# Four v loads issued by GpSimd with a cast in the transfer, in a fused linear-attention and snake-MLP kernel

## The chip, the cores and the metric

The kernel runs on one core of one Trainium2 chip. The metric is the time of one execution on the device in microseconds (us); the median of several executions is compared. TensorE is called PE, VectorE DVE, ScalarE ACT, GpSimd POOL and SyncE SP. SP does nothing but issue transfers (DMAs).

## What is computed

There are two parts, one feeding the other. The first is a linear attention with decay over 4 batches, 8 heads, 768 positions and a head size of 64; the second is a feed-forward network with the snake activation on all 3072 tokens.

```python
# attention; lam: one decay per head
for each block of positions:
    intra = ((q @ k.T) * Dmask) @ v            # Dmask[i, j] = lam ** (i - j) for i >= j, else 0
    inter = (q * lam ** (i + 1)) @ kv_state
    out[block] = intra + inter
    kv_state = lam ** block * kv_state + (k * lam ** (block - 1 - j)).T @ v
# feed-forward, x: [3072, 512]
h = x @ w_in                                   # [3072, 2048]
s = sin(alpha * h)
g = h + s * s / (alpha + 1e-9)
y = g @ w_out                                  # [3072, 512], float32
```

All inputs and the output are float32 in DRAM.

## The kernel before, in words

**Attention.** The 768 positions of a batch are cut into 6 blocks of 128 rows, so there are 24 steps `s` (4 batches of 6). A step loads q, k and v as tiles of 128 rows by 8 heads by 64 (`load_one`, L531, one transfer of 256 KB each, all issued by SP at L543, into the float32 rings `q32`, `k32`, `v32` of six buffers each). A row of such a tile is gathered from eight runs of 64 floats (256 B) in DRAM, one for each head. For the first nine steps (`NPQ`) q has its rows in another order, so that its runs are 1 KB long. Then:

- `prep` (L636) multiplies k and q by powers of lam and writes bfloat16 tiles (`k{s}` at L641, `q{s}` at L647 or L650), on DVE or POOL.
- `T{s}` transposes both on PE (L678, L681) into PSUM, and a copy `tc{s}` brings them to `qkT`; later steps transpose by a DMA instead (`DT{s}`).
- `S{s}` multiplies q with k (L699) into `A_ps`, and DVE multiplies by the mask (`mask{s}`, L703).
- `prep_v` (L659) casts v from `v32` into the bfloat16 ring `v2` of five buffers: `v{s}`, through the helper at L619. This runs on the engine that the table `ENG` names: v0 and v2 on DVE, v1 and v3 on ACT, v4 on POOL.
- `O{s}` adds the state's part (L721, from `Zs`) and the part of this block (L725), `x{s}` copies the result to `xT`, `Z{s}` (L745) updates the state with k and v, and `zs{s}` copies it to `Zs`.

**Feed-forward.** Six chunks of four steps (512 tokens) each. `A{c}.{m}` (L770) is one of 16 groups of 128 hidden columns of chunk c: matmuls, then the sine on ACT (L776), a square `sq` (L781 or L782) on POOL, DVE or ACT, and a fused multiply-add on DVE (L785) into `gT`. A group needs the weights of its columns and the `x` of all four steps of its chunk. `B{c}.{s4}.{m4}` (L801) is a quarter of the second product for one step's 128 tokens. The weights come in sixteen blocks of 512 KB, `w0` to `w7` of w_in and `w8` to `w15` of w_out (`w_block`, L621): a load on SP (L631) into a ring `wst` of five float32 buffers, and a cast `wc{j}` at L619 to bfloat16 on POOL, DVE or ACT.

**Order.** Three things set it. `LOADS` is the order in which SP issues the loads; it begins

```python
    "k0 q0 v0 k1 q1 k2 q2 k3 q3 v1 v2 q4 v3 w0 k4 w1 q5 w2 w3 w4 w5 k5 w6 w7 w8 w9 v4 w10 w11 k6 q6 q7 w12 "
```

`SCRIPT` is the order of PE's work: the attention of steps 0 to 3 with a few idle matmuls (`w1`, `warm`, L842) between them, then the first chunk `A0.0`, `A0.1`, with T4 and S4 among them, and so on. For DVE, ACT and POOL the program makes its own plan: each operation is recorded with what it reads and writes and with an expected duration, and `schedule` (L216) goes through them in expected time. For each engine it takes the operation that can begin first, among those of equal time the one of higher priority, and then the one that PE needs soonest:

```python
                    k = (t, o.prio, o.need, o.idx)
                    if c is None or k < c[0]:
                        c = (k, o, dur)
```

An operation that may run on several engines goes where it is expected to end first, unless `ENG` names an engine for its tag. Transfers are planned by a model of three queues (`Transfers`, L116) that share the DMA engines when more than one of them is busy. `emit` (L355) then writes each engine's instructions in the planned order, with semaphore waits where an operation depends on another. The instructions of an engine run in that order.

POOL starts with the constants (`consts`, L546): one small transfer of lam (`lam_sb`, L565), then five selects that make the identity and mask tiles (`ident`, `identP`, `identf`, `maskP`, `mask`) and three iotas. `mask` is read from step 9 on only; the first nine steps use `maskP`.

Of the kernel before, what the change touches and what calls it, by code (L numbers as in the profile page):

```python
# [38 lines left out]
)  # L39
BIAS_DVE, BIAS_ACT, BIAS_W = (0.3, 0.3, 0.3)  # L40
NPQ, NW, FETCH = 9, 5, 1.2
ENG = {
    "k0": "DVE",
    "k1": "DVE",
# [122 lines left out]
class Program:  # L167
# [10 lines left out]
    def add(self, engs, fn, dur=0.0, reads=(), writes=(), slot=None, work=0.0, after=(), prio=0, tag="",  # L178
            insts=0):
        if isinstance(engs, str):  # L180
            engs = ((engs, dur),)
        elif tag in ENG:
            engs = tuple(x for x in engs if x[0] == ENG[tag])
            call = fn
            fn = lambda e: call(e, ENG[tag])
        op = Op(engs, fn, len(self.ops))
# [236 lines left out]
def bass_lightning_attn__then__act_snake_kernel(  # L423
# [25 lines left out]
    RC = 5  # L449
# [6 lines left out]
    with es:  # L456
# [3 lines left out]
        def ring(name, n, shape, dt):  # L460
            return [sb(f"{name}_{i}", shape, dt) for i in range(n)]
# [10 lines left out]
        v2 = ring("v2", RC, [128, H, D], BF16)  # L472
# [45 lines left out]
        rec = P.add  # L518
# [10 lines left out]
        loads = {}  # L529

        def load_one(nme, s):  # L531
            src, dst = {"k": (k, k32), "q": (q, q32), "v": (v, v32)}[nme]
            b, n, r = s // NB, s % NB, s % RL
            work = 1.19
            d = dst[r][:, :, :]
            if nme == "q" and s < NPQ:
                a = bass.AP(q.tensor, b * H * S * D + n * BL * D,
                            [[4 * D, 32], [2 * S * D, 4], [S * D, 2], [1, 4 * D]])
                d = bass.AP(dst[r], 0, [[H * D, 128], [4 * D, 2], [1, 4 * D]])
                work = 0.74  # L540
            else:
                a = src[b, :, n * BL:(n + 1) * BL, :].rearrange("h p d -> p h d")
            loads[nme, s] = rec("SP", lambda e: e.dma_start(d, a), 0, writes=[f"{nme}32.{r}"],  # L543
                                slot=f"{nme}{r}", work=work, tag=f"L{nme}{s}")

# [72 lines left out]
        def copy_of(e, name, out_ap, in_ap):  # L618
            return e.copy(out_ap, in_ap) if name == "ACT" else e.tensor_copy(out_ap, in_ap)  # L619
# [37 lines left out]
                    tag=f"DT{s}")  # L657

        def prep_v(s):  # L659
            r, c = s % RL, s % RC  # L660
            rec((("ACT", 0.61), ("POOL", 0.74, 0.2), ("DVE", 0.52, 0.3)),
                lambda e, name: copy_of(e, name, v2[c][:, :, :], v32[r][:, :, :]),
                reads=[f"v32.{r}"], writes=[f"v2.{c}"], tag=f"v{s}")
# [41 lines left out]

        def att_O(s, own):
            prep_v(s)
            n, c, j, jq = s % NB, s % RC, s % 2, s % NQ
            if not own:
# [141 lines left out]
        def more_loads():  # L851
            while queue and (queue[0][0] == "w" or queue[0][1] < RL or (queue[0][0], queue[0][1] - RL) in used):
                if queue[0][0] == "w":
                    w_block(queue.pop(0)[1])
                else:
                    load_one(*queue.pop(0))
# [4 lines left out]
        for what in SCRIPT.split():  # L861
            a = what[0]
# [56 lines left out]
```

## Time and profile before

| | |
|---|---|
| median of 8 runs | 220.18 us (219.75 to 220.71) |
| profiled execution | 220.69 us |
| its span, first to last instruction | 218.9 us |
| PE busy | 205.0 us (94%) |
| DVE busy | 148.4 us (68%) |
| ACT busy | 136.5 us (62%) |
| POOL busy | 62.4 us (29%) |
| moved by DMA | 37.76 MB, mean 173 GB/s |
| SP's queue (q1), share of the 16 engines | 67.0% |
| GpSimd's queue (q0), share of the 16 engines | 0.2%, 32 packets |

A busy share is an average over stages that have different limits; what a change in one stage is worth is read from that stage. A transfer's row on SP, ACT or POOL is its issue alone; the data land later. In the profile's tables "releaser" or "<-" names what an engine waited for. The stretches below are given in us from the start of the span.

### The profile page before, as it was taken

How to read it: one execution, taken by the hardware profiler on the slowest of the kernel's cores; microseconds unless marked ns; L12 is line 12 of the kernel's file. 1: busy time of each engine (PE TensorE's matmuls, PEld its weight loads, DVE VectorE, ACT ScalarE, POOL GpSimd, SP SyncE). 2: the span in 40 equal slices, each digit the busy share in tenths (PEclk: the TensorE clock that was granted, in tenths of full speed). 3: DMA queues.
4: the chain of work that ended last, by engine and by line, in shares of the span. 5: the costliest groups of instructions: out<-in, count | busy, mean ns of one | idle time of the engine just before them, and what ended most of it. 6: DMA issues, size and time to landing. Idle time of an engine off the chain costs nothing.

```text
span 218.9 us, 3772 instructions
## 1 busy us (share of the span) xinstructions
PE 205.0 (94%) x1483; PEld 101.5 (46%) x1510; DVE 148.4 (68%) x227; ACT 136.5 (62%) x232; POOL 62.4 (29%) x73
## 2 busy tenths in 40 slices
PE   5885897999999999999999999999999999999995
PEld 1353443445544545445454544455444444444453
DVE  3588596956797875689898867887473778536002
ACT  2665699723689855788868855876734777524020
POOL 4262657450437821238254214010000000000000
PEclk9999999999999999999999999999999999999999
DMA  4999999999999999998999999331101110012023
GB/s 85 259 266 290 337 327 348 336 262 275 253 292 210 232 207 202 259 252 156 238 193 222 224 167 252 73 92 9 48 3 48 48 48 3 0 48 96 0 99 144
DMA packets 94034, 37.76 MB, mean 173 GB/s; under 512 B 82352, under 2 KB 89024, under 8 KB 94016
## 3 DMA queue, kind: packets, MB, share of 16 engines
q1 hardware_dynamic: 90352, 31.33, 67.0%
q10 hardware_dynamic: 3632, 6.17, 8.1%
q8 instruction: 12, 0.20, 0.4%
q0 software_dynamic: 32, 0.00, 0.2%
q14 instruction: 6, 0.05, 0.1%
HBM read 27.28 MB, written 6.29 MB: 153 GB/s over the span
## 4 chain that ended last, share of the span: by engine, by line
PE 81%; DMA 7%; SPq 6%; DVE 2%; issue 2%; POOL 1%
PE m_ps L801 37%; PE m_ps L770 33%; DMA wst<-in_moe_w_in_dram 7%; SPq L543 6%; PE A_ps L699 3%; PE A_ps L725 2%; PE m_ps L823 2%; DVE gT L785 2%; PE m_ps L725 1%; POOL w L619 1%; PE A_ps L721 1%; PE Z_ps L745 1%; PE m_ps L721 1%; POOL u L782 0%; PE A_ps L681 0%
## 5 line engine op out<-in xcount | busy, mean ns | idle before, releaser
L770 PE MATMUL m_ps<-xT,w 128*128 128x512 bf16 x369 | 89.9, 379 | 4.4 <-POOL w L619 1.6
L801 PE MATMUL m_ps<-w,gT 128*128 128x512 bf16 x358 | 87.0, 379 | 1.2 <-issue 0.6
L776 ACT ACTIVATE t<-m_ps,alpha_sb 128x512 bf16<-128x512 f32 x96 | 64.8, 685 | 34.4 <-PE m_ps L770 33.7
L785 DVE SCALAR_TENSOR_TENSOR gT<-u,r_sb,m_ps 128x512 bf16<-128x512 bf16 x96 | 69.8, 744 | 9.5 <-ACT u L781 4.5
L770 PEld LDWEIGHTS m_ps<-xT,w 128*128 128x128 bf16 x384 | 35.5, 98 | 44.2 <-POOL w L619 1.8
L801 PEld LDWEIGHTS m_ps<-w,gT 128*128 128x128 bf16 x368 | 34.6, 98 | 41.0 <-DVE gT L785 0.7
L782 DVE TENSOR_TENSOR u<-t 128x512 bf16<-128x512 bf16 x40 | 17.6, 441 | 19.7 <-ACT t L776 19.5
L781 ACT ACTIVATE u<-t 128x512 bf16<-128x512 bf16 x45 | 28.1, 630 | 1.2
L703 DVE TENSOR_TENSOR S_m<-A_ps,mask 128x1024 bf16<-128x1024 f32 x15 | 18.3, 1223 | 6.3 <-PE A_ps L699 6.1
L619 ACT COPY osb<-m_ps 128x512 f32<-128x512 f32 x18 | 10.5, 584 | 14.2 <-PE m_ps L801 14.1
L782 POOL TENSOR_TENSOR u<-t 128x512 bf16<-128x512 bf16 x11 | 11.4, 1039 | 24.5 <-ACT t L776 24.5
L641 POOL TENSOR_TENSOR qk<-k,Lk 128x512 bf16<-128x512 f32 x11 | 11.9, 1083 | 17.4 <-DMA k<-in_k_dram 17.4
L650 POOL TENSOR_TENSOR qk<-q,Lq 128x512 bf16<-128x512 f32 x11 | 13.1, 1198 | 8.8 <-DMA q<-in_q_dram 8.8
L619 DVE COPY osb<-m_ps 128x512 f32<-128x512 f32 x5 | 3.5, 692 | 14.1 <-PE m_ps L801 14.1
L619 ACT CAST Zs<-Z_ps 64x256 bf16<-64x256 f32 x27 | 9.9, 365 | 4.6 <-PE Z_ps L745 3.1
L641 DVE TENSOR_TENSOR qk<-k,Lk 128x512 bf16<-128x512 f32 x13 | 10.1, 776 | 3.5 <-ACT Lk L561 2.6
L842 PE MATMUL m_ps<-zeros,ident 128*128 128x512 bf16 x27 | 9.7, 491 | 2.5 <-POOL ident L583 2.5
L619 POOL CAST w<-wst 128x1024 bf16<-128x1024 f32 x9 | 9.5, 1056 | 7.6 <-DMA wst<-in_moe_w_in_dram 7.6
L703 DVE TENSOR_TENSOR S_m<-A_ps,maskP 128x1024 bf16<-128x1024 f32 x9 | 11.0, 1217 | 0.7 <-PE A_ps L699 0.7
L647 POOL TENSOR_TENSOR qk<-q,L 128x512 bf16<-128x512 f32 x8 | 8.6, 1074 | 9.7 <-DMA q<-in_q_dram 6.3
L699 PE MATMUL A_ps<-qkT 64*128 64x128 bf16 x192 | 9.5, 219 | 1.4 <-DVE S_m L703 1.0
L699 PEld LDWEIGHTS A_ps<-qkT 64*128 64x128 bf16 x192 | 5.4, 94 | 10.0 <-issue 6.7
(73 smaller groups left out, 125.0 us busy)
## 6 DMA issues: line engine op xcount, KB each, us to landing
k<-in_k_dram SPq DMA_DIRECT2D x24, 256.0 KB, 5.0
q<-in_q_dram SPq DMA_DIRECT2D x24, 256.0 KB, 5.3
v<-in_v_dram SPq DMA_DIRECT2D x24, 256.0 KB, 5.1
out_dram<-osb ACTq DMA_DIRECT2D x23, 256.0 KB, 2.8
wst<-in_moe_w_in_dram SPq DMA_DIRECT2D x8, 512.0 KB, 7.6
wst<-in_moe_w_out_dram SPq DMA_DIRECT2D x8, 512.0 KB, 7.6
qkT<-qk SPq DMA_TRANSPOSE x15, 4.0
out_dram<-osb ACTq DMA_DIRECT2D x1, 128.0 KB, 1.8
```

Of the source, the lines that this page charges most:

```text
L543: loads[nme, s] = rec("SP", lambda e: e.dma_start(d, a), 0, writes=[f"{nme}32.{r}"], slot=f"{nme}{r}", work=work, tag=f"L{nme}{s}")
L619: return e.copy(out_ap, in_ap) if name == "ACT" else e.tensor_copy(out_ap, in_ap)
L641: rec(two, lambda e, _: e.tensor_tensor(k2[c], k32[r][:, :, :], Lk_b, ALU.mult), reads=[f"k32.{r}", "Lk"], writes=[f"k2.{c}"], tag=f"k{s}")
L650: rec(two, lambda e, _: e.tensor_tensor(q2[c], q32[r][:, :, :], Lq_b, ALU.mult), reads=[f"q32.{r}", "Lq"], writes=[f"q2.{c}"], tag=f"q{s}")
L699: last = e.matmul(A_ps[:, 4 * h + jp, :], qkT[j][rows, 4 + jp, :], qT(s, rows, jp))
L703: rec("DVE", lambda e: e.tensor_tensor(S_m[j2][:, :, :], A_ps[:, :, :], mask_b, ALU.mult), 1.22, reads=["S0", "S1", "maskP" if s < NPQ els ...
L770: last = e.matmul(m_ps[i][:, 0:n], w1[:, kc, 128 * m:128 * (m + 1)], xT[x][:, kc, 0:n], start=(kc == 0), stop=(kc == NKC - 1))
L776: rec("ACT", lambda e: e.activation(t16[tt][:, 0:n], m_ps[i][:, 0:n], ACTF.Sin, scale=alpha_sb[:, m:m + 1]), 0.27 + 0.41 * f, reads=[f"m.{ ...
L781: return e.activation(u16[tt][:, 0:n], t16[tt][:, 0:n], ACTF.Square)
L782: return e.tensor_tensor(u16[tt][:, 0:n], t16[tt][:, 0:n], t16[tt][:, 0:n], ALU.mult)
L785: rec("DVE", lambda e: e.scalar_tensor_tensor(out=gT[g][:, m, 0:n], in0=u16[tt][:, 0:n], scalar=r_sb[:, m:m + 1], in1=m_ps[i][:, 0:n], op0 ...
L801: last = e.matmul(m_ps[bank][:, :], gT[g][:, m, 128 * s4:128 * (s4 + 1)], w2[:, m, :], start=(m == 0), stop=(m == NM - 1))
```

## The change

For the first four steps (`NSV = 4`) v is no longer loaded as float32 by SP and cast by an engine. Instead POOL issues a transfer that reads the float32 v from DRAM and writes bfloat16 straight into the tile `v2` of that step; the transfer has its own four semaphores (`sv0` to `sv3`). The planner is told 1.4 us of POOL for the issue and the same work on the DMA engines as before. `prep_v` has nothing to do for these steps. SP's list of loads is walked through as before, without v0, v1, v2 and v3. The steps from 4 on are as they were, and `LOADS`, `SCRIPT` and `ENG` are unchanged.

```diff
 NPQ, NW, FETCH = 9, 5, 1.2
+NSV = 4
 ENG = {
...
                 a = src[b, :, n * BL:(n + 1) * BL, :].rearrange("h p d -> p h d")
+            if nme == "v" and s < NSV:
+                loads[nme, s] = rec("POOL", lambda e: e.dma_start(v2[s % RC][:, :, :], a), 1.4, writes=[f"v2.{s % RC}"],
+                                    slot=f"sv{s % RC}", work=1.19, tag=f"L{nme}{s}")
+                return
             loads[nme, s] = rec("SP", lambda e: e.dma_start(d, a), 0, writes=[f"{nme}32.{r}"],
                                 slot=f"{nme}{r}", work=work, tag=f"L{nme}{s}")
...
         def prep_v(s):
+            if s < NSV:
+                return
             r, c = s % RL, s % RC
             rec((("ACT", 0.61), ("POOL", 0.74, 0.2), ("DVE", 0.52, 0.3)),
                 lambda e, name: copy_of(e, name, v2[c][:, :, :], v32[r][:, :, :]),
```

## The prediction

> **What bounds the kernel now.** I read the page's slices first, then the chain of waits, then the busy time by stage, then the rows of the engines that the change touches. The slices show two regimes: TensorE (PE) is at 9 tenths from the eighth slice on, and in the slices before that it is the DMA engines that are full.
>
> ```profile
> PE   5885897999999999999999999999999999999995
> DMA  4999999999999999998999999331101110012023
> GB/s 85 259 266 290 337 327 348 336 262 275 253 292 210 232 207 202 259 252 156 238 193 222 224 167 252 73 92 9 48 3 48 48 48 3 0 48 96 0 99 144
> ```
>
> The chain of waits says which transfers matter. From 14 us to 42 us it is these pieces (start, length, what):
>
> ```profile
> 14.23 7.17 DMA wst<-in_moe_w_in_dram
> 21.40 0.05 issue
> 21.46 1.05 POOL w L619
> ...
> 27.48 7.62 DMA wst<-in_moe_w_in_dram
> 35.09 0.05 issue
> 35.15 1.21 POOL w L619
> 36.36 1.01 POOL u L782
> ```
>
> So the first feed-forward group (A0.0, 22.55) waits for weight block w0, landing at 21.40, and the stall around 37 to 38 us goes back to w7, landing at 35.09. Both transfers were issued over 7 us before they landed: they stand behind everything queued ahead of them. Busy time by stretch (PE, PEld, DVE, ACT, POOL, clock, DMA share, GB/s):
>
> ```profile
> 3.00:5.20 2.20, 2.20 (x7) 0.79 (x6) 0.70 (x3) 0.21 (x1) 0.75 (x4) 1.00 0.77 155
> 5.20:12.00 6.80, 5.77 (x40) 2.44 (x37) 4.22 (x5) 4.05 (x9) 2.11 (x3) 1.00 1.08 259
> 12.00:20.00 8.00, 5.93 (x103) 4.01 (x104) 7.00 (x11) 5.27 (x10) 3.82 (x4) 1.00 1.13 264
> 23.00:28.00 5.00, 4.95 (x36) 2.45 (x36) 3.54 (x6) 4.19 (x7) 2.58 (x3) 1.00 1.03 343
> 54.00:57.00 3.00, 2.84 (x44) 1.86 (x46) 2.56 (x5) 1.32 (x3) 1.66 (x2) 1.00 1.16 224
> ```
>
> Weights run at 343 GB/s (1 KB runs), the q, k and v loads around 55 us at 224 GB/s (all of 256 B runs there), each with the engines full. After 42.2 us PE is busy 171.7 of 176.7 us; what the start wins or loses, the end wins or loses.
>
> **What the Trainium skill says.** "DMA: Bandwidth & Descriptors", section Issuing engines are not separate DMA queues: transfers started by SP, ACT or GpSimd run on the same 16 engines and interleave, so a second issuer saves only issue time. The trace agrees as far as it can: SP needs 0.59 us for the issue of v0, far less than the load's landing time, 5.1 us in the median. The same page, SWDGE vs HWDGE vs iDMA: a cast in the transfer is only possible from GpSimd, where software writes the descriptors. The trace has one such issue, without a cast (lam_sb, 0.77 us). "Perfetto Trace Analysis", DMA Instruction — SWDGE (GPSIMD): the row of such an issue ends when the last descriptor is written, not when data has moved; lam_sb shows it, 0.77 us of row and 4.8 us to landing. "SBUF — State Buffer", section SBUF: two separate sides: a VectorE operation in a two-port mode keeps GpSimd from writing descriptors. No row of before shows this; VectorE's only v cast in the stretch, at 8.52 us, is one that the change removes.
>
> **The change, part by part.** *Removed casts.* v0 and v2 on DVE, v1 and v3 on ACT:
>
> ```profile
> 8.52 0.41 DVE L619 CAST v<-v 128x512 bf16<-128x512 f32 x1
> ...
> 17.40 0.93 DVE L619 CAST v<-v 128x512 bf16<-128x512 f32 x1
> 18.25 1.21 DVE L703 TENSOR_TENSOR S_m<-A_ps,maskP 128x1024 bf16<-128x1024 f32 x1
> ```
>
> ACT's two (0.62 us each) stand in idle stretches. DVE's second one stands ahead of mask3: S3 ended at 17.61, so mask3 could begin about 0.6 us earlier, and with it O3 and x3, which ends at 21.41. But A0.0 begins only after the cast of w0 ends at 22.50: x3 already has 1.1 us of slack. Worth at A0.0: 0.
>
> *Four issues off SP.* They cost SP 0.59, 2.56 for two, and 0.60 us: 3.75 us. w0's issue at 14.23 goes to about 10.5. Its landing isn't set by that but by the engines ahead: 7.17 us lie between the two. Worth by itself: 0. Later SP runs sooner into the ring of five weight buffers (w7 uses the buffer of w2, cast at 26.00 to 27.04); it then waits longer there, with several us of transfers still queued. Cost 0 while that backlog lasts; were it gone, w7 couldn't start before 27.1.
>
> *Four issues on POOL.* POOL is free from 3.74 (end of the mask select) to 7.01 and from 8.05 to 10.56:
>
> ```profile
> 3.46 0.28 POOL L586 TENSOR_SCALAR_AFFINE_SELECT mask<-maskf 128x128 bf16<-128x128 f32 x1
> 7.01 1.04 POOL L647 TENSOR_TENSOR qk<-q,L 128x512 bf16<-128x512 f32 x1 [3.26 <-ACT Lk L561]
> 10.56 1.04 POOL L641 TENSOR_TENSOR qk<-k,Lk 128x512 bf16<-128x512 f32 x1 [2.50 <-DMA k<-in_k_dram]
> ```
>
> The planner takes, of the operations ready at one time, the one that PE needs first; the loads need nothing, so they go behind the maskP select (ends 3.50) and ahead of `mask`, which is used only from step 9 on. Each has 128 x 8 runs, 1,024, against 128 for lam_sb. Price: at least lam_sb's 0.77 us; at most eight times that, 6.2; I take the 1.4 that the diff gives the planner. 3.5 + 4 x 1.4 = 9.1 us, before k2's scaling at 10.56, whose data landed only then. Cost 0; up to 1.75 us each it would be hidden. What stands in the way is q0's scaling at 7.01: the planner, seeing POOL taken, will give it to DVE behind k0. k0 took 1.50 us beside POOL's q0 and k1 alone 0.68, so k0 and q0 in turn on DVE take about 1.4 us where they took 1.5 side by side. T0 (8.71) stays.
>
> *The transfers.* The same 4 x 256 KB are read. A v at 224 GB/s occupies the engines for 262,144 / 224e3 = 1.17 us, four for 4.7 us, all of them before w0 in either kernel. Can a second queue fill gaps? k0 to k4, v0 to v3 at 224 and q0 to q4 (1 KB runs) at 343 GB/s need 9 x 1.17 + 5 x 0.76 = 14.3 us for 3.67 MB: 256 GB/s. The stretches 5.2 to 20 already run at 259 and 264. The gap is before 5.2 us (155 GB/s), and v0 issued at 3.5 comes too late for it: lam_sb landed 4.8 us after its issue. The planner itself assumes that two queues together run 1.09 times as fast; over some 9 us of two queues that would be 0.8 us. A cast's descriptors don't appear in the trace: bounds are 0.8 us gained in all (the planner's factor), and, if each costs twice a plain one because the cast runs in the path, 4.7 us lost. I take 0.
>
> *Order.* POOL's loads take engine turns from k1 to q3. At worst all four v pass ahead of q3, which v1 to v3 followed before: 3 x 1.17 = 3.5 us. q3's scaling goes from 13.90 to about 17.4, T3 from 15.22 to 18.5, and T3 to the end of x3 took 6.2 us with DVE's queue in between, about 4.6 at bare durations (T3 0.60, copy 1.01, S3 0.40, mask3 1.22, O3 0.75, x3 0.59): 23.1, against 22.50 for w0's cast: 0.6 us at worst, and nothing at a fair share, where q3 comes 1 to 2 us later. I take 0. New waits: PE at O0 to O3 waits for the v transfer instead of a cast; behind it stand the next S and T, and DVE's mask after them. O0 (13.84) has several us to spare; O1 to O3 likewise.
>
> *Replanning.* The planner assigns many later operations by its own times, which shift by some tenths; I put that at 0 with 0.4 us either way, half of one scaling or cast (0.7 to 1.0 us on DVE and POOL) coming onto the path or leaving it.
>
> Sum: 0 at the casts, 0 at SP, 0 at POOL, 0 at the engines: the profiled execution of 220.69 us (span 218.9 and 1.8 around it) would come out at 220.7. It lies 0.5 us above the median of the eight runs; against that median the forecast is **220.2 us**.
>
> **The rivals.** *R1, slower: the cast's descriptors are dear on the DMA engines.* Place: the engines before w0 and w7. For: runs of 256 B are already the least efficient kind (224 against 343 GB/s), and the written runs become 128 B. Against: the same number of runs is moved. Price at half as much again: 4 x 0.59 = 2.3 us later at w0 and w7, with nothing between to absorb it (PE idles only 1.7 us from 22.55 to 42.2): 222.5. It decides from 1.28 us a load on (0.44 us in all).
>
> *R2, slower: writing 1,024 descriptors holds POOL.* At 2.5 us each v3's issue ends at 13.5; k2 and q2 come 3 us late, T2 to x3 with them; less 1.1 us of slack and the 0.6 us of the cast gone, A0.0 is 1.3 us late: 221.5. It decides from some 2.3 us each (3.5 + 4 x 2.3 = 12.7, over 10.56 by 1.7 and 0.44). Against: 1.4 is well under that.
>
> *R3, faster: two queues do run better than one.* For: the DMA share goes to 1.13 where packets overlap, so a share of 1 is no ceiling. Against: the even mix rate above. Up to 0.8 us at w0 and w7, and x3 (ahead by 0.6) allows it: 219.4.
>
> *R4: nothing but the replanning*, 219.8 to 220.6; this has the forecast's time and counts with it.
>
> **How the numbers follow.** 0.2% of 220 us, 0.44 us, is about what a measurement of this kernel can tell from no change. Forecast with R4: 0.38, of which 0.28 lie within 0.44 us, 0.04 below and 0.06 above. R1: 0.25. R2: 0.14. R3: 0.23. Faster 0.27, same 0.28, slower 0.45. For 8 in 10: R3's full size and a little replanning give 219.2; R1 at half as much again with 0.3 us of replanning gives 222.8. The forecast's own range is 219.7 to 220.7.
>
> **What would show it.** Right: four POOL issue rows of about 1.4 us from 3.5 to 9.1; q0 on DVE; w0 landing within 0.4 us of 21.40 and w7 of 35.09; x3 ending near 21 and A0.0 near 22.5. R1: the GpSimd queue's share of the engines well over 4 x 1.17 / 219 = 2.1%, w0 and w7 late alike. R2: rows over 2.3 us, k2's scaling late. R3: w0 and w7 both early, and more GB/s from 5 to 20 us. Wrong altogether would be a change that first appears after 45 us.

## The result: slower by 1.1%, and the profile after

| | before | after |
|---|---|---|
| median | 220.04 us (32 runs) | 222.51 us (11 runs, 221.5 to 224.0) |
| ratio | | 1.0108 (95% interval 1.0086 to 1.013) |
| profiled execution | 220.69 us | 221.18 us |
| its span | 218.9 us | 219.3 us |

Each ratio in what follows is to the runs of before made on the same chip beside it. The profiled execution of after is the quickest of its twelve (the median is over the other eleven), so its trace shows where the start changes, not the whole 2.5 us. The slices, in the form in which the prediction shows those of before:

```profile
PE   5666899999999999999999999999999999999994
PEclk9997999999999999999999999999999999999999
DMA  4999999999999999999999999230101110012023
GB/s 89 218 275 329 334 317 337 357 232 246 256 303 204 230 189 188 257 246 198 203 206 199 243 176 223 48 91 11 48 3 48 48 48 3 0 48 96 0 99 143
```

A slice is 5.5 us. The second and third digits of PE were 8 and are now 6: PE does less between 5.5 and 16.4 us; in the fourth slice its clock is down to 7 tenths. The DMA engines are as full as they were, yet GB/s falls in the second slice (259 to 218) and rises in the fourth (290 to 329). The stretches of the start, with the columns of the prediction, say the same: 
```profile
5.20:12.00 6.80, 4.74 (x40) 2.19 (x37) 3.64 (x5) 4.08 (x9) 3.12 (x5) 1.00 1.62 216
12.00:20.00 8.00, 4.58 (x80) 3.30 (x80) 5.32 (x9) 2.34 (x5) 4.59 (x7) 0.94 1.22 300
```

PE was busy for 5.77 and 5.93 us in them and is now for 4.74 and 4.58. The transfers with the cast count in GB/s by what they write, 128 KB, not by the 256 KB they read, so the 216 looks worse than it is. By bytes read (each v counted as 256 KB), before had moved some 4.3 MB by 20 us and after some 4.8 MB. Something arrives earlier, and something later. The chain of waits says which of the two sets the time (start, length, what):

```profile
7.12 8.59 DMA k<-in_k_dram
15.71 0.07 issue
15.78 1.04 POOL qk L646
16.82 1.01 POOL qk L652
17.83 0.04 issue
17.88 0.40 PE m_ps L685 x4
...
18.71 0.22 PE m_ps L728 x4
...
20.54 0.58 PE m_ps L728 x4
...
22.94 0.38 PE m_ps L728 x4
23.32 0.36 PE m_ps L732 x8
23.68 0.02 issue
23.70 0.59 ACT xT L624
24.30 0.14 issue
24.43 1.02 PE m_ps L777 x4
```

Before, the piece that ended last ahead of A0.0 was weight block w0. Now it is k3: landed at 15.7, scaled on POOL (L646), then q3 behind it on the same engine (L652), then T3 (L685) at 17.88. The three rows of L728 are O1, O2 and O3: they stand behind T3 in PE's order, one after another through the state. x3 ends at 24.29, and A0.0 begins at 24.43. POOL's timeline shows the issues and the two scalings (start, length, what, in brackets the idle time before it and what ended it):

```profile
3.48 3.60 POOL L545 DMA_DIRECT2D v<-in_v_dram  x4
...
11.07 1.04 POOL L646 TENSOR_TENSOR qk<-k,Lk 128x512 bf16<-128x512 f32 x1 [3.69 <-DMA k<-in_k_dram]
...
15.78 1.04 POOL L646 TENSOR_TENSOR qk<-k,Lk 128x512 bf16<-128x512 f32 x1 [2.94 <-DMA k<-in_k_dram]
16.78 2.04 POOL L652 TENSOR_TENSOR qk<-q,L 128x512 bf16<-128x512 f32 x2
18.77 1.04 POOL L624 CAST w<-wst 128x1024 bf16<-128x1024 f32 x1
```

The four issues take 0.90 us each and end at 7.08; after the `mask` select POOL idles until k2 lands. The last row is w0's cast: it begins at 18.77, not at 21.46, and A0.0 no longer waits for it. Landings and PE's milestones of the two profiled executions (a landing is the issue plus the time to landing in the DMA view):

| us | before | after | |
|---|---|---|---|
| k2, q2 landed | 10.5, 11.9 | 11.0, 13.4 | +0.5, +1.5 |
| k3, q3 landed | 13.0, 13.8 | 15.7, 16.4 | +2.7, +2.5 |
| T3 begins | 15.22 | 17.88 | +2.7 |
| w0, w7 landed | 21.4, 35.1 | 18.7, 31.9 | -2.7, -3.2 |
| A0.0 begins | 22.55 | 24.43 | +1.9 |
| A0.15 begins | 42.21 | 42.58 | +0.4 |
| A5.15 begins | 199.53 | 199.91 | +0.4 |

So the q and k loads of steps 2 and 3 come later, the weights earlier. A0.0 loses 1.9 us to the first; the second gives 1.5 us back by A0.15, because the wait for w7 is gone. That the median lies 2.5 us over that of before, and this execution only 0.5 us over the profiled one of before, is taken up below.

### The profile page after: what moved, and what is told of

It is laid out like the page before. It is cut to its first block, busy times and chain, and to the rows that moved or that the text cites. A ratio compares the mean times of both kernels' runs of the same rounds, so it can differ in the third digit from the quotient of the medians.

```text
span 219.3 us, 3768 instructions
## 1 busy us (share of the span) xinstructions
PE 204.9 (93%) x1483; PEld 102.1 (47%) x1510; DVE 150.8 (69%) x226; ACT 133.4 (61%) x228; POOL 66.0 (30%) x78
## 4 chain that ended last, share of the span: by engine, by line
PE 84%; DMA 4%; ACT 3%; SPq 3%; DVE 3%; issue 2%; POOL 1%; DVEq 0%
PE m_ps L808 36%; PE m_ps L777 35%; DMA k<-in_k_dram 4%; SPq L548 3%; PE A_ps L706 3%; PE m_ps L732 2%; PE A_ps L732 2%; PE m_ps L830 2%; DVE gT L792 2%; PE m_ps L728 1%; ACT t L783 1%; ACT u L788 1%; PE Z_ps L752 1%; PE A_ps L728 1%; PE m_ps L849 1%
## 5 line engine op out<-in xcount | busy, mean ns | idle before, releaser
L789 DVE TENSOR_TENSOR u<-t 128x512 bf16<-128x512 bf16 x45 | 22.3, 498 | 21.4 <-ACT t L783 21.0
L788 ACT ACTIVATE u<-t 128x512 bf16<-128x512 bf16 x41 | 25.5, 628 | 1.0
L624 ACT COPY osb<-m_ps 128x512 f32<-128x512 f32 x20 | 11.7, 585 | 15.6 <-PE m_ps L808 15.6
L646 POOL TENSOR_TENSOR qk<-k,Lk 128x512 bf16<-128x512 f32 x14 | 14.8, 1065 | 15.9 <-PE Z_ps L752 8.9
L655 POOL TENSOR_TENSOR qk<-q,Lq 128x512 bf16<-128x512 f32 x11 | 12.4, 1131 | 13.2 <-DMA q<-in_q_dram 13.2
L624 DVE COPY osb<-m_ps 128x512 f32<-128x512 f32 x3 | 2.1, 692 | 13.4 <-PE m_ps L808 13.4
L849 PE MATMUL m_ps<-zeros,ident 128*128 128x512 bf16 x27 | 8.9, 454 | 2.5 <-POOL ident L588 2.5
L624 POOL CAST v<-v 128x512 bf16<-128x512 f32 x10 | 6.6, 670 | 15.0 <-DMA v<-in_v_dram 13.7
L624 ACT CAST xT<-m_ps 128x512 bf16<-128x512 f32 x8 | 4.7, 586 | 10.7 <-PE m_ps L732 10.6
```

Of the source, the lines that this page charges most:

```text
L646: rec(two, lambda e, _: e.tensor_tensor(k2[c], k32[r][:, :, :], Lk_b, ALU.mult), reads=[f"k32.{r}", "Lk"], writes=[f"k2.{c}"], tag=f"k{s}")
L655: rec(two, lambda e, _: e.tensor_tensor(q2[c], q32[r][:, :, :], Lq_b, ALU.mult), reads=[f"q32.{r}", "Lq"], writes=[f"q2.{c}"], tag=f"q{s}")
L788: return e.activation(u16[tt][:, 0:n], t16[tt][:, 0:n], ACTF.Square)
L789: return e.tensor_tensor(u16[tt][:, 0:n], t16[tt][:, 0:n], t16[tt][:, 0:n], ALU.mult)
L849: last = e.matmul(m_ps[bank][:, :], ident[:, :], zeros[:, :])
```

## The experiments

TURNS is the theory that follows: the two queues take turns on the DMA engines, the v loads (needed late) pass the k and q loads (needed early), and A0.0 waits for x3. Its rivals are dear casts, the fall of the PE clock (0.94 between 12 and 20 us) and the new plan.

### The same loads without the cast

```diff
-                loads[nme, s] = rec("POOL", lambda e: e.dma_start(v2[s % RC][:, :, :], a), 1.4, writes=[f"v2.{s % RC}"],
+                loads[nme, s] = rec("POOL", lambda e: e.dma_start(d, a), 1.4, writes=[f"v32.{r}"],
...
         def prep_v(s):
-            if s < NSV:
-                return
```

> v0 to v3 are still issued by POOL, but as float32 into v32, and the four casts on DVE and ACT are back. Theory TURNS (the POOL transfers take engine turns from k2, k3 and q3, so T3 comes late): k3's scaling again starts between 14.5 and 16 us, T3 between 17 and 18.5, and the time is 222 to 223.5. Theory DEAR CASTS (the converting descriptors cost the engines more than plain ones): the GpSimd queue's share falls from 3.9% to about 2.2%, k3's scaling starts before 14 us, and the time is 220 to 221.

Measured: 223.54 us, ratio 1.0175 (1.0152 to 1.0199). The casts on DVE and ACT are back here and the plan is another, so the time alone doesn't tell what the cast in the transfer costs. Where the k loads land tells more: DEAR CASTS expected k3's scaling before 14 us, and k3 landed at 17.0. TURNS had the direction, but T3 began at 19.44, later than its 17 to 18.5. POOL's queue in the page of after (packets, MB, share of 16 engines), and the same line of this kernel:

```profile
q0 software_dynamic: 4192, 0.53, 3.9%
```

```profile
q0 software_dynamic: 352, 1.05, 2.3%
```

With the cast each run of 64 numbers is a packet of its own, 128 B written; without it the packets are of some 4 KB. The k2 load on the other queue, issued at 4.2 us in both, landed at 11.0 in after and at 14.8 here, as POOL's scaling of it shows:

```profile
14.90 1.04 POOL L646 TENSOR_TENSOR qk<-k,Lk 128x512 bf16<-128x512 f32 x1 [7.51 <-DMA k<-in_k_dram]
```

The Trainium skill ("DMA: Bandwidth & Descriptors", section Queues, rings and completion order) says that an engine goes round its queues a whole packet at a time. Larger packets on POOL's side would then take more of each round from SP's; the 3.8 us by which k2 came later agree with that, though the transfers alone (below) show far less of it.

### Two loads issued later

```diff
-                                    slot=f"sv{s % RC}", work=1.19, tag=f"L{nme}{s}")
+                                    slot=f"sv{s % RC}", work=1.19, after=[loads["q", 2]] if s > 1 else [], prio=-1 if s > 1 else 0, tag=f"L{nme}{s}")
```

> The change, with v2 and v3 issued by POOL only when q2 has landed. TURNS: with two loads instead of four beside k2 to q3, k3's scaling starts at 13.5 to 14.5 us instead of 15.8, T3 by 16.2, and the time is 219.5 to 221. DEAR CASTS: the same descriptors are spent before w0, the weights land as in the change, and the time is 222 or more. The planner puts k3 on DVE here, which may help T3 by up to 1 us of its own; e4_pins measures that.

Measured: 224.99 us, ratio 1.0245 (1.0223 to 1.0267). The first half of TURNS came true: k3 landed at 13.5 and T3 began at 15.79. The time, for which it had 219.5 to 221 us, did not follow, because v2 and v3 and their consumers came late. In the chain of waits:

```profile
12.67 7.31 DMA v<-in_v_dram
19.98 0.05 issue
20.03 0.40 PE m_ps L728 x4
...
22.18 2.11 issue
24.29 0.59 PE m_ps L728 x4
```

The last two rows are O3: v3, issued at 13.61, landed at 24.2, though the profile doesn't name it as what ended that wait. A0.0 began at 26.18. The two loads took 7.3 and 10.6 us to land, so "later" was too late. The experiment confirms what delays k3 and refutes the cure.

### The PE clock

Eleven more idle matmuls ahead of T2 and T3, in after:

```diff
-    ... S1 t2 w1 o0 S2 t3 w1 o1 ...
+    ... S1 w5 t2 w1 o0 S2 w6 t3 w1 o1 ...
```

> The change, with five and six more idle matmuls (w5, w6) on PE ahead of T2 and T3, where PE stood idle. Theory CLOCK (much of the loss is the half-speed stretch that follows PE's idle gaps at 12.5 to 17.9 us): the granted clock stays at 1.0 until the end, the runs scatter less, and the median comes to 220.5 to 221.5. Theory TURNS ALONE (the late T3 is all of it): the clock may stay up, but the median is 222 to 223.5, the added matmuls (11 at 0.22 us, 2.4 us) filling idle time at best.

Measured: 223.51 us, ratio 1.0171 (1.0149 to 1.0194). The clock was 1.0 in every run, where in after it is 0.983 to 1.0 in the mean of a run. The time did not improve. The plan changed with it, so the trial was repeated with the plan held (below).

### Two scalings put on the engines that had them

k3's scaling back on DVE and q2's on POOL, as before the change:

```diff
 ENG = {
...
+    "k3": "DVE",
+    "q2": "POOL",
```

> The change, with k3 held on DVE and q2 on POOL as in the kernel before. Theory PLAN (the planner's new assignment, k3 and q3 one after the other on POOL, is the main loss): T3 starts 1 us or more earlier than 17.9 and the time is 220 to 221. TURNS: k3 still lands at 15 to 16 us, T3 gains at most the 1 us of q3's waiting behind k3, and the time is 221.5 to 223.

Measured: 221.27 us, ratio 1.0067 (1.0041 to 1.0092). The time lies between the two forecasts. In the profiled execution, the slowest of the six (222.18 us), k3 landed at 15.7 as in after and T3 began at 17.65, only 0.2 us earlier. The two scalings seem to be worth some 0.4%, but not by way of T3.

### The plan of before, kept exactly

Here the planner plans the kernel before. Afterwards the four v loads are put on POOL behind the `maskP` select, their casts are dropped, and the users of a cast wait for the load; every other instruction keeps its engine and its place.

```diff
+    def moved(self, order):
+        by = {o.tag: o for o in order}
+        casts = {by[f"v{s}"]: by[f"Lv{s}"] for s in range(NSV)}
...
+            if o in moved or o in casts:
+                continue
+            out.append(o)
+            if o.tag == "maskP_sel":
+                out += list(casts.values())
...
-        order = self.schedule()
+        order = self.moved(self.schedule())
```

> The four transfers alone: every engine keeps the order and the engine choices that the planner made for the kernel before; only the four loads go to POOL behind the maskP select and the four casts are dropped. TURNS: k3 lands at 15 to 16 us as in the change, T3 starts near 16.8 (k3 on DVE, q3 on POOL), the granted clock halves for 3 to 7 us, and the time is 220.8 to 222. REPLANNING (the new plan is the main loss): the time is at or below the kernel before, 219 to 220.2, since w0 and w7 land some 3 us earlier.

Measured: 221.5 us, ratio 1.0066 (1.0045 to 1.0088). With the old plan the change costs 0.7%, and the new plan about 0.4% more; the two intervals just overlap (1.0088 and 1.0086), but the kernel with the two scalings put back lies as low (1.0067). k3 landed at 15.7 here too, and what stands behind it is now on DVE:

```profile
15.68 0.69 DVE L671 TENSOR_TENSOR qk<-k,Lk 128x512 bf16<-128x512 f32 x1 [3.21 <-DMA k<-in_k_dram]
16.29 1.22 DVE L733 TENSOR_TENSOR S_m<-A_ps,maskP 128x1024 bf16<-128x1024 f32 x1
```

DVE idles 3.21 us for k3 while mask1 (L733), whose S1 was done at 13.27, waits behind it in DVE's order. S2 waits for mask1's PSUM tile, T3 begins at 17.98, A0.0 at 24.42: the same two places as in after, by another route.

With the plan held and the idle matmuls added (11 ahead of T2 and T3, not known to the planner):

> f1_frozen with five and six idle matmuls on PE ahead of T2 and T3 that the planner doesn't count, so that the plan stays as it was. CLOCK: the granted clock stays at 1.0 and the time is 0.7 to 1.5 us below f1_frozen. TURNS ALONE: the clock stays up and the time is within 0.4 us of f1_frozen.

Measured: 221.88 us, ratio 1.0102 (1.0075 to 1.0129), the clock 0.999 to 1.0 in five of six runs (the sixth: 0.992, 223.7 us). So idle matmuls are no cure. But that doesn't show that the low clock costs nothing, since they stood in the way themselves. First the kernel without them, then the one with them:

```profile
17.98 0.60 PE L708 MATMUL m_ps<-identP,qk 128*128 128x128 bf16 x4
...
24.42 1.02 PE m_ps L800 x4
```

```profile
17.60 1.47 PE L872 MATMUL m_ps<-zeros,ident 128*128 128x512 bf16 x6
18.91 0.39 PE L708 MATMUL m_ps<-identP,qk 128*128 128x128 bf16 x4
...
24.32 1.02 PE m_ps L800 x4
```

Without them the clock is at half from 18.03 to 21.44, and A0.0 begins 6.44 us after T3; with them it is full, and A0.0 begins 5.41 us after T3, but T3 waits 0.9 us longer, behind the last six. The one about pays for the other. The other runs of the kernel without them leave the clock as a suspect: the two with a mean clock of 0.998 and 1.0 took 219.86 and 220.32 us, about as long as before (219.92 on that chip), the nine at 0.991 or 0.992 221.3 in the mean, the three at 0.984 or 0.985 222.6. Even before, on another chip, took 221.5 in the mean of five runs at 0.991 or 0.992 and 220.0 in thirty at 0.999 or 1.0. This is a correlation: a run in which k3 lands later would have more idle time and a lower clock alike. How much of the loss is the clock's stays open.

### How many v loads: two, one and three

The same kernel with `NSV = 2` (v0 and v1 on POOL, v2 and v3 on SP with their casts), 1 and 3.

```diff
-NSV = 4
+NSV = 2
```

> f1_frozen with v0 and v1 alone on POOL; v2 and v3 are loaded by SP at their old places and cast as before. TURNS: half as many turns are taken, k3 lands at 13.8 to 14.6 us, T3 starts by 16, w0 still lands 1 to 2 us early, and the time is 219 to 220. If any software queue at all costs the start more than its turns (DEAR CASTS, or POOL held), the time is half way between the kernel before and f1_frozen.

> f1_frozen with v0 alone on POOL. TURNS: k3 lands at 13 to 13.6 us, T3 starts at 15.2 to 15.5, w0 lands 0.5 to 1 us early, the clock stays at 1.0, and the time is 219.4 to 220. DEAR CASTS or POOL held: a quarter of the way from the kernel before to f1_frozen.

> f1_frozen with v0, v1 and v2 on POOL and v3 on SP. TURNS with DVE's queue behind k3: k3 lands between f3_frozen_v2's 13.3 and f1_frozen's 15.7 us, at about 14.5; mask1, queued behind k3's scaling on DVE, starts about 1 us later than in f3_frozen_v2 (13.95), and the time is 219.5 to 220.8. If the loss of the fourth load were its own (POOL's ring full, v3 late), this kernel would be as fast as f3_frozen_v2, 218.9.

| v loads on POOL | k3 landed | T3 | w0 landed | A0.0 | median us | ratio to before |
|---|---|---|---|---|---|---|
| 0 (before) | 13.0 | 15.22 | 21.4 | 22.55 | 220.04 | 1 |
| 1 | 13.0 | 15.31 | 21.1 | 22.29 | 219.67 | 0.9986 (0.9974 to 0.9998) |
| 2 | 13.3 | 15.55 | 18.6 | 21.35 | 218.90 | 0.9964 (0.9949 to 0.9979) |
| 3 | 14.5 | 16.83 | 18.8 | 22.56 | 219.73 | 0.9976 (0.9955 to 0.9996) |
| 4 | 15.7 | 17.98 | 18.8 | 24.42 | 221.50 | 1.0066 (1.0045 to 1.0088) |

With the plan held, this table is the answer to where the time went. Going from 1 to 2, w0 comes 2.5 us earlier and k3 hardly later; from 2 on each further load delays k3 by 1.2 us and A0.0 by 1.2 and 1.9 us, and w0 has nothing more to give. The 0.7 us that the last step has on top lie behind T3: A0.0 begins 5.80 and 5.73 us after it with two and three loads, at full clock, and 6.44 with four, where the clock is halved. A loss in proportion to the number of loads, as DEAR CASTS or a held POOL would have it, isn't there: one, two and three loads are no slower than none. With two loads the kernel is faster than both versions. Its chain of waits:

```profile
7.07 6.25 DMA k<-in_k_dram
...
20.62 0.60 ACT xT L649
21.22 0.14 issue
21.35 1.02 PE m_ps L800 x4
```

k3 takes 6.25 us to land instead of 8.59, and A0.0 begins at 21.35, right after x3 and 1.2 us earlier than in before; w0 is no longer the limit.

Two loads with the planner's own plan (`NSV = 2` in after):

> The change with NSV = 2, planned by the planner itself. It puts k3 and q3 one after the other on POOL as in the change. TURNS: k3 lands at 13.3 us as in f3_frozen_v2, T3 comes about 1 us later than its 15.55, and the time is 219 to 220. REPLANNING as a loss of its own, apart from k3 and q3: 220 or more.

Measured: 219.9 us, ratio 0.9994 (0.997 to 1.0017). T3 began at 15.28, not 1 us late as TURNS had it, and A0.0 at 20.82, earlier still. But in the profiled execution (220.73 us, 0.8 us above the median) the lead over before, 1.2 us at S6 (47.40 against 48.58), was gone by S8 (62.66 against 62.64). Against the old plan with the same transfers the planner's new plan again seems to cost some 0.3% (the intervals just overlap), this time later in the kernel.

### The transfers alone

Six loads at a time on one queue or two, with nothing else in the kernel:

> Transfers alone; no attention and no feed-forward are computed, and the output is zeros. Six loads of v at a time: by SP as float32, by POOL as float32, by POOL with the cast; then six k by SP beside six v by POOL with the cast, and beside six v by POOL as float32. TURNS: the three kinds take 1.0 to 1.3 us a load alone; beside POOL casts an SP load takes about twice its time alone, beside POOL float32 loads much longer, since there POOL's packets are of 4 KB (80 packets a load in e1_plain, 1040 in the change). DEAR CASTS: a cast load alone takes 1.8 us or more, and the k loads take longer beside the casts than beside the float32 loads.

The columns by stretch are its bounds, its length, the busy time of DVE and of POOL, the clock, the DMA share and GB/s; the lines are SP alone, POOL without a cast, POOL with it, SP beside POOL with it, and SP beside POOL without it:

```profile
2.50:9.00 6.50, 0.00 (x0) 0.00 (x0) 1.00 1.28 226
12.00:18.00 6.00, 0.00 (x0) 3.33 (x4) 1.00 0.98 229
22.00:27.00 5.00, 0.00 (x0) 3.13 (x4) 1.00 1.98 126
31.00:43.00 12.00, 0.00 (x0) 3.05 (x4) 1.00 1.61 168
47.00:60.00 13.00, 0.00 (x0) 3.43 (x4) 1.00 1.16 222
```

126 GB/s written are 252 read: a cast is no dearer than a plain load of the same runs (226, 229), though its DMA share reads 1.98. Together the queues read 224 GB/s (168 counted, in which every 256 KB of plain load stand beside 128 KB written by a cast that read 256), and 222 without the cast, as one alone. So runs of 256 B gain nothing from a second queue. In the last two stretches SP's loads landed 8.1 and 9.1 us after their issue in the median, against 4.6 alone. About twice the time is what TURNS expected; "much longer" beside plain loads didn't come, so the size of the packets explains only a part of k2's 3.8 us, if any. This, too, is one execution. What remained was the gain that after does show by 20 us, with its q and weights of 1 KB runs. Four stretches of 3.15 MB read each:

```diff
+            for i in range(4):                                  # 3: v and w on SP
+                SP.dma_start(v3[i][:, :, :], src(v, i)).then_inc(sem["d"], 16)
+                wload(SP, w3[i], i).then_inc(sem["d"], 16)
...
+            for i in range(4):                                  # 4: w on SP beside v with the cast on POOL
+                wload(SP, w4[i], i).then_inc(sem["e"], 16)
+                G.dma_start(v4[i][:, :, :], src(v, i)).then_inc(sem["f"], 16)
```

> Only transfers, in four stretches that each read 3.15 MB, each begun after the one before has landed; everything else is left out and the output is zeros. Stretch 1: four k, four q (1 KB runs) and four v in turn on SP's queue. Stretch 2: the same k and q on SP, the four v by POOL with the cast. Stretch 3: four v and four weight blocks in turn on SP's queue. Stretch 4: the weight blocks on SP, the four v by POOL with the cast. TWO QUEUES MOVE MORE (the mix of long runs on SP's queue with short ones on GpSimd's lets the engines move more, which the run with 256 B runs alone could not show): stretch 2 is at least 8% shorter than stretch 1 and stretch 4 at least 8% shorter than stretch 3, from first issue to last landing, as the kernel after had read 4806 KB by 20 us where the kernel before had read 4283. NO MORE BY ITSELF: 1 and 2, and 3 and 4, agree within 4% (12.5 to 13 us each at 250 GB/s), and what the kernel after gained by 20 us comes from elsewhere (its order, or the gaps in SP's issues).

The stretches from first issue to last landing (their length is the second number): k, q, v on SP; k, q beside v on POOL; v and weights in turn on SP; weights beside v on POOL:

```profile
0.74:15.17 14.43, 0.48 (x1) 0.00 (x0) 1.00 1.00 218
15.19:29.88 14.69, 0.00 (x0) 3.65 (x4) 1.00 1.19 179
29.90:43.86 13.96, 0.00 (x0) 0.00 (x0) 1.00 0.80 225
43.88:55.68 11.80, 0.00 (x0) 3.50 (x4) 1.00 1.26 222
```

Each theory got one half: beside k and q nothing is gained (14.69 against 14.43 us), beside weights 2.2 us of 14.0 are (11.80 against 13.96). The DMA share (the last column but one) says where there was room: 1.00 with k, q and v on SP alone, but 0.80 with v and weights in turn. It is one execution. It fits after, whose last v landed at 15.5 with w0 already issued at 10.35. It does not explain the kernel with two loads, where both v had landed by 11.4, before w0 was issued at 12.95, and w0 still came at 18.6. Why that kernel gains as much stays open.

## Why the prediction was right and wrong

The forecast of no change was wrong: 222.51 us against 220.2. That the time lies inside the stated range of 219.2 to 222.8 is luck, since its upper end came from R1 (R2 reached 221.5), and neither rival happened. By its steps:

- **Removed casts, issues off SP, issues on POOL: right.** The POOL issues ended at 7.08, with 0.90 us each instead of 1.4; w0's issue moved from 14.23 to 10.35 (10.5 was named); q0 went to DVE, and k0 beside nothing took 0.69 us. None of them lies on the path.
- **R2, descriptor writing holds POOL: excluded** by the 0.90 us, against the 2.3 from which it would decide.
- **R1, dear descriptors: excluded.** Its mark, a share of POOL's queue well over 2.1%, did appear (3.9%); its place did not, since w0 and w7 came earlier. The run with the transfers alone shows that the share misleads: 252 GB/s read with the cast. Plain loads in the kernel cost more (1.0175).
- **Order: the step that failed.** It named the right mechanism and even a T3 of 18.5 at worst (17.88 measured), and then took it at nothing. Two of its terms were mis-sized. The "fair share" delay of q3, "1 to 2 us", measured 2.5, and k3, which it left out, 2.7. And "about 4.6 at bare durations" from T3 to the end of x3 measured 6.41 (17.88 to 24.29): the list of durations holds step 3 alone, while PE's order has O1 and O2, and the state copies between them, behind T3, and PE ran at half clock from 19.03 to 22.45. With 6.2 us, the figure that it had read from the trace and set aside, 17.88 gives 24.1, 1.6 us past w0's cast at 22.50.
- **The transfers: mis-sized, R3 was right in kind.** Put at 0, with 0.8 us as the bound of R3; w0 came 2.7 and w7 3.2 us earlier. The bound was a factor from the planner, not a reading. Without this gain the loss would have been larger: in the profiled execution it gave back 1.5 of 1.9 us by A0.15.
- **Replanning: mis-sized.** 0 with 0.4 us either way; the kernel with the old plan held shows about 0.9 us (0.0108 less 0.0066, of 220 us), with intervals that just overlap. Where it lies isn't shown: q3 in turn behind k3 on POOL takes 1.01 us in the chain, but with the old plan T3 and A0.0 begin as late (17.98 and 24.42).
- **The PE clock** wasn't in the prediction. It did fall to half for 3.4 us. The idle matmuls that held it up gained nothing in all, but with the plan held they cost about as much ahead of T3 as the full clock saved behind it.

The sum of what is measured: some 1.5 us for the change with the old plan, by way of k3, T3 and x3 and with a share of the clock in it that is not separated, and some 0.9 us for the new plan. What stays open: the profiled execution of after ends only 0.5 us later than that of before, so some 1.3 us of the median's loss are in no trace. Its other runs, at mean clocks of 0.983 to 1.0, took 221.5 to 224.0 us. Part of it may be a longer stretch at half clock: six runs at 0.983 to 0.985 took 222.9 us in the mean, the five at 0.992, the profiled one among them, 222.1, and in the kernel with the two scalings put back a profile at 0.985 shows the clock at half for 6.8 us (16.78 to 23.61). The difference of 0.65 us between before's own profile and its median is the other part of that gap.

## What to carry to other kernels

A second DMA queue added no room beside the q and k loads, and only some beside weights; what it did above all was to let its transfers pass those of the first. Before moving loads, list by deadline what they will overtake, move only as many as leave the early ones in place (here two of four, 0.9964 against 1.0066), and follow a delay through everything that stands behind it in each engine's order, not only its own step, with a look at the clock of the stretch in which PE has to catch up. When a program plans by itself, hold the old plan to separate the edit from the replanning.

## What the runs showed of the hardware

- A GpSimd issue of 1,024 runs held POOL for 0.90 us, with or without the cast; `lam_sb` with 128 runs took 0.77. Eight times the runs cost 0.13 us more.
- A cast on the way in cost no bandwidth (252 GB/s read, in one execution). Beside its small packets the other queue's loads landed earlier than beside plain 4 KB ones: k2 at 11.0 against 14.8 us in the kernel, and 8.1 against 9.1 us after their issue with the transfers alone.
- A GpSimd load issued beside SP's landed 6.7 to 9.3 us later in after, and 7.3 and 10.6 us later where two were held back; alone the medians were 4.2 us with the cast and 4.6 without.
- The Trainium skill ("DMA: Bandwidth & Descriptors", section Rules for kernel authors) says that spreading transfers over the issuing engines doesn't help bandwidth. That held for k, q and v (14.43 and 14.69 us) but not for weights beside v: 13.96 against 11.80 us; so far as one execution goes, the measurement decides.
- After PE had idled 1.25 us ahead of T2 and 1.55 ahead of T3, the granted clock fell to half for 3.4 us in after (19.03 to 22.45). With the old plan it was 1.58 us ahead of T2 and 1.50 ahead of S2, then half clock from 18.03 to 21.44, in which the four matmuls of a transpose took 0.60 us instead of 0.40.
